# Query projections of an attention block in six groups of 8 or 12 heads instead of eight groups of 8

## The chip, the cores and the metric

The kernel runs on one core of one Trainium2 chip (trn2). The metric is the time of one execution on the device, in microseconds (us), as the median of repeated runs.

## The reference

A layer norm, sliding-window attention over a cache, and a gated FFN are combined. x has 2048 rows of 448.

```python
xn = layernorm(x)
q = (xn @ wq)                          # 448 -> 16 heads x 256
k, v = last 512 rows of the cache      # 8 key/value heads, each used by 2 query heads
s = softmax(q k^T / 16) v @ wo         # attention, 4096 -> 448
g = silu((gelu(xn @ w_gate) * (xn @ w_up)) @ w_down)
out = x + s * g
```

The rows are handled in four chunks of 512, so attention is 4 x 16 = 64 "chunk heads" (called heads below). The contraction of the projections is 448 = 3 x 128 + 64.

## The kernel before

Everything is laid out so that TensorE never waits. The gate and up matmuls of the FFN come first. Attention then alternates between *projection phases*, which make queries for a group of heads, and a *stream* in which each head's scores are followed by the P·V product of the head two places earlier.

The projections use **half-height** matmuls: two of them, on rows 0 to 63 and 64 to 127 of the array, run at the same time into two banks of PSUM, the memory that matmuls write to. This avoids padding 448 to 512. Scores, P·V, output projection and down projection use the full 128 rows.

```python
HG = 8                                   # heads of a group
# half-height pairs: u picks the rows 0-63 or 64-127, j the bank
for u, j in ((0, ph), (1, 1 - ph)):
    rows = slice(R * u, R * u + R)       # R = 64
    l = wr[rows] if k == NK else w(j, k)[rows]
    lst.append((bank[b + j][:, lo:hi], l, xnT[rows, k, cols], ...))
# ...
for c in range(NQC):                     # 4 chunks
    for g in range(NG):                  # 2 groups of 8 heads
        h0 = g * HG
        # ... (set-up at the very first group)
        for i in range(0, HG, 2):        # projection phase
            q_group(c, h0 + i, (cur, nxt)[i // 2 % 2])
        # ... (buffers released after the very first phase)
        for i in range(HG):              # stream
            s_mm(h0 + i)                 # scores, exponentials, transposes of one head
            # ... (down projections of the last two chunks at the very first heads)
            if len(late) == LAG:         # LAG = 2
                pv(late.pop(0))          # P.V of the head two back
            # ... (output projection of the last chunk after the second head of a chunk)
            late.append(h0 + i)
```

Queries lie in 8 slots (`qT`) of 2 KB per partition. The softmax of a head is 4 exponentials on ScalarE, 4 reciprocals and 4 scalings on VectorE, and 2 DMA transposes of the probabilities (`pT<-pn`).

The softmax here doesn't subtract the row's maximum and nothing guards it: scores larger than these inputs give would overflow.

## Time and profile before

| | |
|---|---|
| time, median (6 runs) | 557.23 us (556.96 to 557.56) |
| span of the profiled run | 555.1 us |
| first instruction to first query matmul | 114.035 us |
| first query matmul to start of the last output-projection matmul | 437.474 us |
| rest | 3.577 us |

The last three rows are differences of start times in the trace; "rest" runs to the end of the span. From the profile page, here are the head, the slices of TensorE and its clock, and the chain of waits:

```profile
span 555.1 us, 9781 instructions
...
PE 549.7 (99%) x3651; PEld 260.1 (47%) x3651; DVE 317.0 (57%) x817; ACT 273.9 (49%) x727; POOL 32.9 (6%) x64
...
PE   8999999999999999999999999999999999999997
...
PEclk9999999999999999999999999999999999999999
...
PE 98%; DVE 0%; DMA 0%; issue 0%
```

TensorE bounds the kernel. But "busy" cannot show how much of that time is useful: a 128x512 matmul lasts 379 ns in the trace and the next one starts well before it ends. These are three of its largest groups in attention (busy us, mean ns of one, idle before it):

```profile
L327 PE MATMUL bank<-kT,qT 128*128 128x512 bf16 x512 | 121.0, 379 | 0.0
L327 PE MATMUL bank<-pT,va 128*128 128x512 bf16 x512 | 120.8, 379 | 0.0
L327 PE MATMUL bank<-xnT,wq 64*128 64x512 bf16 x768 | 94.7, 376 | 0.0
```

All report an idle time of 0.0, also the first matmuls of a phase. The starts tell more. This is the timeline of TensorE around one projection phase (start us, length us, instruction, how many), cut in its middle:

```profile
168.13 1.89 PE L327 MATMUL bank<-kT,qT 128*128 128x512 bf16 x8
169.86 1.89 PE L327 MATMUL bank<-pT,va 128*128 128x512 bf16 x8
171.68 0.82 PE L327 MATMUL bank<-xnT,wq 64*128 64x512 bf16 x6
...
182.49 1.46 PE L327 MATMUL bank<-xnT,wq 64*128 64x512 bf16 x12
183.88 1.90 PE L327 MATMUL bank<-kT,qT 128*128 128x512 bf16 x8
185.61 1.67 PE L327 MATMUL bank<-pT,va 128*128 128x512 bf16 x7
```

Subtract the start of one line from the start of the next. Eight score matmuls take 169.86 - 168.13 = 1.73 us, 216 ns each. (The Trainium skill, "TensorE: Matmul & The Clock Gate", section "Wait — 56ns, not 53.3ns?", gives N / 2.4 GHz + about 2.5 ns for N columns, and 215.7 ns as measured at 512; this trace agrees, with 215.83 ns over 125 steps, from 184.3 to 211.3 us.) The eight P·V matmuls before the projection take 171.68 - 169.86 = 1.82 us, so 0.09 us is lost. The last 12 half-height matmuls are 6 pairs and should take 6 x 0.216 = 1.30 us; they take 183.88 - 182.49 = 1.39 us, so another 0.09 us is lost. About 10 ns more goes at the second matmul after each change. The whole is 213 or 214 ns at every phase but the first, which comes after other half-height matmuls and loses 105 ns at its exit only.

### The profile page before, as it was taken

Reading aid. Unit: us, or ns where it says so; the run is one execution under the profiler, and the core shown is the slowest. Engines: PE = TensorE matmul, PEld = TensorE weight load, DVE = VectorE, ACT = ScalarE, POOL = GpSimd, SP = SyncE. Lnnn points to the kernel's source line nnn. Section 1 sums busy time; section 2 is a strip of 40 time slices with the busy share of each in tenths; the row PEclk is TensorE's granted clock in tenths of the full one; section 3 lists DMA queues with packets and bytes.
Section 4 is the critical chain, followed back from the end, with each engine's and each line's share of the span. In section 5 each row is a group of like instructions: output and inputs, shape, how many; then the busy total and the mean of one; then the engine's idle time right before and its main releaser. Section 6 shows DMA issues by size and latency. Waiting matters only on the chain.

```text
span 555.1 us, 9781 instructions
## 1 busy us (share of the span) xinstructions
PE 549.7 (99%) x3651; PEld 260.1 (47%) x3651; DVE 317.0 (57%) x817; ACT 273.9 (49%) x727; POOL 32.9 (6%) x64
## 2 busy tenths in 40 slices
PE   8999999999999999999999999999999999999997
PEld 6444444444544444454444445544444454444455
DVE  6773534443485785525858752285785525858722
ACT  5432324353485784505758751085784504758600
POOL 1120830000000000000000000000000000000000
PEclk9999999999999999999999999999999999999999
DMA  9560799703175383313706803176364313707601
GB/s 302 104 164 9 199 277 297 108 1 39 38 134 96 76 149 81 76 35 90 153 20 152 152 21 74 34 145 100 77 151 77 77 34 90 153 20 152 153 8 34
DMA packets 163599, 57.63 MB, mean 104 GB/s; under 512 B 151456, under 2 KB 160672, under 8 KB 163552
## 3 DMA queue, kind: packets, MB, share of 16 engines
q1 hardware_dynamic: 159488, 45.16, 39.9%
q0 software_dynamic: 3296, 11.27, 6.9%
q8 instruction: 29, 0.48, 0.4%
q10 hardware_dynamic: 768, 0.57, 0.3%
q14 instruction: 18, 0.15, 0.1%
HBM read 17.92 MB, written 1.84 MB: 36 GB/s over the span
## 4 chain that ended last, share of the span: by engine, by line
PE 98%; DVE 0%; DMA 0%; issue 0%
PE bank L327 98%; DMA x<-in_A_x_dram 0%; DVE stats L375 0%; PE bank L426 0%; DVE xn L401 0%; DVE mv L378 0%; PE bank L445 0%; DVE tmp L679 0%; DVE ofin L682 0%; DVE rstd L395 0%
## 5 line engine op out<-in xcount | busy, mean ns | idle before, releaser
L640 ACT ACTIVATE p<-bank 128x512 f32<-128x512 f32 x256 | 149.5, 597 | 103.0 <-PE bank L327 99.9
L644 DVE TENSOR_SCALAR pn<-p,rden 128x512 bf16<-128x512 f32 x256 | 124.5, 486 | 16.4 <-DMA pT<-pn 7.6
L327 PE MATMUL bank<-kT,qT 128*128 128x512 bf16 x512 | 121.0, 379 | 0.0
L327 PE MATMUL bank<-pT,va 128*128 128x512 bf16 x512 | 120.8, 379 | 0.0
L327 PE MATMUL bank<-wo,oT 128*128 128x448 bf16 (+2 forms) x544 | 97.7, 341 | 0.0
L327 PE MATMUL bank<-xnT,wq 64*128 64x512 bf16 x768 | 94.7, 376 | 0.0
L327 PE MATMUL bank<-xnT,wgu 64*128 64x512 bf16 (+1 forms) x780 | 83.6, 347 | 0.4 <-issue 0.3
L327 PEld LDWEIGHTS bank<-pT,va 128*128 128x128 bf16 x512 | 50.0, 98 | 60.5 <-DMA pT<-pn 0.7
L327 PEld LDWEIGHTS bank<-kT,qT 128*128 128x128 bf16 x512 | 49.5, 98 | 61.6 <-issue 3.4
L327 PEld LDWEIGHTS bank<-wo,oT 128*128 128x128 bf16 x544 | 52.0, 98 | 45.5
L626 DVE CAST qT<-bank 128x512 bf16<-128x512 f32 x64 | 42.8, 691 | 49.4 <-PE bank L327 49.4
L321 ACT ACTIVATE qT<-bank 128x512 bf16<-128x512 f32 x64 | 38.2, 597 | 61.1 <-PE bank L327 59.5
L327 PEld LDWEIGHTS bank<-xnT,wq 64*128 64x128 bf16 x768 | 36.8, 94 | 46.8 <-ACT p L640 2.1
L321 ACT ACTIVATE gl<-bank 128x512 bf16<-128x512 f32 x56 | 33.1, 597 | 49.8 <-PE bank L327 46.6
L494 DVE TENSOR_TENSOR actT<-bank,gl 128x512 bf16<-128x512 f32 x56 | 37.8, 689 | 34.0 <-PE bank L327 25.3
L327 PEld LDWEIGHTS bank<-xnT,wgu 64*128 64x128 bf16 x780 | 35.3, 94 | 39.0 <-issue 1.3
L643 DVE RECIPROCAL rden<-rsum 128x1 f32<-128x1 f32 x256 | 40.3, 157 | 21.9 <-ACT p L640 21.8
L640 ACT ACTIVATION_READ_ACCUMULATOR p<-bank 128x1 f32 x256 | 52.8, 206 | 0.0
L679 DVE SCALAR_TENSOR_TENSOR tmp<-bank,g 128x448 f32<-128x448 f32 (+2 forms) x17 | 10.1, 596 | 72.2 <-PE bank L327 72.2
L663 DVE CAST oT<-bank 128x512 bf16<-128x512 f32 x64 | 43.7, 683 | 6.9 <-PE bank L327 6.9
L327 PE MATMUL bank<-wd,actT 128*128 128x448 bf16 x224 | 43.0, 353 | 0.0
L321 ACT ACTIVATE oT<-bank 128x512 bf16<-128x512 f32 x64 | 39.2, 612 | 7.0 <-PE bank L327 7.0
(39 smaller groups left out, 183.6 us busy)
## 6 DMA issues: line engine op xcount, KB each, us to landing
wo<-in_A_wo_dram POOLq DMA_DIRECT2D x4, 896.0 KB, 21.0
wq<-in_A_wq_dram POOLq DMA_DIRECT2D x2, 1536.0 KB, 11.4
va<-in_A_v_cache_dram POOLq DMA_DIRECT2D x8, 256.0 KB, 16.6
pT<-pn SPq DMA_TRANSPOSE x128, 2.8
xr<-in_A_x_dram POOLq DMA_DIRECT2D x16, 112.0 KB, 2.3
out_dram<-ofin SPq DMA_DIRECT2D x15, 112.0 KB, 1.7
wd<-in_B_w_down_dram SPq DMA_DIRECT2D x1, 1568.0 KB, 8.3
x<-in_A_x_dram SPq DMA_DIRECT2D x2, 448.0 KB, 5.5
```

What stands on the lines that cost most here:

```text
L321: K.op("act", lambda e, o=o, i=i: e.activation(o, i, func, scale=scale), reads, writes)
L327: ins = e.matmul(o, lhsT=l, rhs=r, start=st, stop=sp)
L494: K.op("dve", lambda e: e.tensor_tensor(actT[:, c % 2, f, :], bank[b + 1], gl[:, s, :], ALU.mult), (b_ps[b + 1], b_gl[s]), (b_actT[c % 2][ ...
L626: K.op("dve", lambda v, s=s, b=b: v.tensor_copy(qT[:, s, 1, :], bank[b + 1]), (b_ps[b + 1],), (b_qT[s][1],))
L640: K.op("act", lambda e, b=b, r=r, z=z: e.activation(p32[:, z, :], bank[b], ACT.Exp, scale=att_scale, accum_out=rsum[:, r:r + 1]), (b_ps[b] ...
L643: K.op("dve", lambda e, r=r: e.reciprocal(rden[:, r:r + 1], rsum[:, r:r + 1]), (b_rsum[r],), (b_rden[r],))
L644: K.op("dve", lambda e, r=r, z=z, y=y, t=t4 % 2: e.tensor_scalar(pn[:, y, t, :], p32[:, z, :], rden[:, r:r + 1], None, op0=ALU.mult), (b_p ...
L663: K.op("dve", lambda v, i=i, b=b: v.tensor_copy(oT[:, i, :], bank[b]), (b_ps[b],), (b_oT[i],))
L679: K.op("dve", lambda e: e.scalar_tensor_tensor(out=tmp[:, s, c0:c1], in0=bank[b][:, c0:c1], scalar=0.5, in1=g2[:, t, c0:c1], op0=ALU.mult, ...
```

## The change

The intent was one stream of 64 heads through all chunks. With 12 slots, groups may cross the border between chunks, and there are fewer of them: 8, 12, 12, 12, 12, 8. The four new slots lie on activations of the FFN that have been used by then.

```diff
+    QS = 12
 ...
-        qT, a, at = place("qT", [P, HG, 2, QC], BF16, at=b_gl[0].lo)
+        qT, a, at = place("qT", [P, QS, 2, QC], BF16, at=b_gl[0].lo - (QS - HG) * 2 * QC * 2)
 ...
-        def qs(h):
-            return HG - 1 - h % HG
+        def qs(n):
+            return QS - 1 - n % QS
 ... (q_group, s_mm and pv take the number of the head in the stream)
-        for c in range(NQC):
-            for g in range(NG):
 ...
+        NS = NQC * Hq
+        groups = [0, HG] + list(range(HG + QS, NS, QS)) + [NS]
+        K.reuse([b for y in b_qT[QS - HG:] for b in y])
 ...
+        for m in range(NS):
+            if m in groups:
+                for i in range(m, groups[groups.index(m) + 1], 2):
+                    q_group(i, (cur, nxt)[i // 2 % 2])
 ...
+            s_mm(m)
+            if m < LAG:
+                down(NQC - LAG + m, nxt)
+                if m == LAG - 1:
+                    K.reuse(b_oT + [b for y in b_qT[:QS - HG] for b in y])
+            if len(late) == LAG:
+                pv(late.pop(0))
+            if m > Hq and m % Hq == LAG - 1:
 ...             (output projection of the last chunk, as before)
+            late.append(m)
```

## The prediction

> **What bounds the kernel now.** TensorE. In the table by 10 us windows it is busy for all of every window from 20 to 550 us, at a granted clock of 1.00; the chain of waits is 98% matmuls. Since matmuls overlap, busy alone is weak evidence, so I took start-to-start distances from the timeline. In the stream of scores and P·V, eight 128x512 matmuls take 1.73 us, 216 ns each, one head 3.45 us, and nothing is lost between heads. A projection of queries for 8 heads is 112 half-height matmuls, 56 pairs of 216 ns, 12.08 us.
>
> The only regular loss in attention is at the ends of such a projection. The last P·V matmul before it is followed after 312 ns, not 216, and the step out to the scores loses about as much again. Summed from the last P·V matmul to the second score matmul, 7 of the 8 projections exceed 216 ns per matmul or pair by 215 to 216 ns in all. The first loses 105 ns only, since half-height gate and up matmuls precede it. So regular a loss is no wait for data. It fits the Trainium skill, "TensorEngine Tiling (Array Packing)", Key Properties: changing the tiling mode drains the array. The projection is 64 rows high, everything around it 128.
>
> **What the change does.** Matmuls, evictions, exponentials and transposes stay; only order and slots differ. Eight projection phases (8 heads each) become six (8, 12, 12, 12, 12, 8): two round trips of mode are removed. Nothing is added. Output projections stay after heads 17, 33 and 49. The four extra slots lie on the end of the FFN's activations and are first written for heads 8 to 11, after both last down projections, so nothing new waits.
>
> **On the critical path.** All of it: 2 x 0.216 = 0.43 us. Longer streams have no idle time to fill: TensorE has no other holes there.
>
> Could streams of 12 heads (41 us) fall behind? Per head, ScalarE does 4 exponentials of 0.60 us and a copy of 0.61, VectorE 4 x (0.16 + 0.49) + 0.68 = 3.3 us, the transposes about 2 x 1.25 us of issue, all below 3.45. From 184 to 211 us ScalarE waits about 0.54 us for TensorE at nearly every head, early and late, so no backlog grows. One late transpose (2.46 us of issue, 5.1 to land) cost TensorE 95 ns at 378 us and was soon made up.
>
> **Predicted time:** 557.23 - 0.43 = 556.8 us; 8 in 10 between 556.2 and 557.5. Faster by over 2%: 0.5%; within 2%: 98.5%; slower by over 2%: 1%.
>
> **What would show it right or wrong.**
> - The span falls by 0.3 to 0.6 us; matmul counts and means stay.
> - Six projection phases; those of 12 heads last 84 pairs x 216 ns = 18.1 us; each of five loses 216 ns at its two ends.
> - In streams of 12 heads eight matmuls still take 1.73 us at the twelfth. VectorE's waits for transposes (7.6 us before) stay of that size and do not reach TensorE.
> - Wrong, if the wait list has TensorE or its weight loads waiting for transposes, exponentials or query copies for whole microseconds, most likely late in a stream or after the second projection.
>
> **What would make it wrong.** Backlog in the softmax chain in longer streams; an order of slots that makes query copies wait; late transposes becoming commoner; or the loss at a phase's ends growing with its length. A gain above 1 us would mean a loss that start-to-start distances don't show me.

## The result and the profile after

The median is 556.86 us (556.47 to 557.55, 6 runs) against 557.23. The ratio is 0.9994, with a 95% interval of 0.9981 to 1.0007. A ratio here is the mean time of one kernel's runs over the mean of the other's in the same rounds, so it is not quite the ratio of the medians. The times by themselves do not separate the two kernels; the traces do.

| from the traces, us | before | after | difference |
|---|---|---|---|
| start to first query matmul | 114.035 | 114.105 | +0.070 |
| first query to last output-projection matmul | 437.474 | 437.008 | -0.466 |
| rest | 3.577 | 3.585 | +0.008 |
| span | 555.086 | 554.698 | -0.388 |

The same parts of the page after the change:

```profile
span 554.7 us, 9768 instructions
...
PE 547.6 (99%) x3626; PEld 260.6 (47%) x3651; DVE 317.1 (57%) x817; ACT 274.1 (49%) x727; POOL 32.9 (6%) x64
...
PE   8999999999999999999999999999999999999997
...
PEclk9999999999999999999999999999999999999999
...
PE 97%; DMA 1%; ACT 1%; issue 0%; DVE 0%; SPq 0%
```

and the three groups:

```profile
L328 PE MATMUL bank<-pT,va 128*128 128x512 bf16 x512 | 120.8, 379 | 0.0
L328 PE MATMUL bank<-kT,qT 128*128 128x512 bf16 x487 | 117.8, 379 | 2.0 <-ACT qT L322 1.0
...
L328 PE MATMUL bank<-xnT,wq 64*128 64x512 bf16 x768 | 94.4, 376 | 0.0
```

Here lies a trap. The score matmuls seem to have become 25 fewer, and TensorE seems to wait 1.0 us for query copies (`qT`). Neither is so. Weight loads (PEld) are 3651 in both kernels, and at each of the 25 places the distance of two neighbours is exactly one matmul longer (216 ns): 25 records are missing from this trace. One of them is the first score matmul after each projection phase, which shows here (timeline of TensorE):

```profile
168.20 1.89 PE L328 MATMUL bank<-kT,qT 128*128 128x512 bf16 x8
169.93 1.89 PE L328 MATMUL bank<-pT,va 128*128 128x512 bf16 x8
171.75 0.82 PE L328 MATMUL bank<-xnT,wq 64*128 64x512 bf16 x6
...
188.60 1.46 PE L328 MATMUL bank<-xnT,wq 64*128 64x512 bf16 x12
190.22 1.67 PE L328 MATMUL bank<-kT,qT 128*128 128x512 bf16 x7 [0.16 <-ACT qT L322]
191.73 1.46 PE L328 MATMUL bank<-pT,va 128*128 128x512 bf16 x6
```

and its weight load is there, at 189.99 us, one of eight (timeline of the weight loads):

```profile
189.99 1.41 PEld L328 LDWEIGHTS bank<-kT,qT 128*128 128x128 bf16 x8 [0.42 <-issue]
```

From 188.60 to 190.22 are 1.62 us: 6 pairs, one matmul without a record, and the same 0.1 us of loss. A phase of 12 heads costs the same at its ends as one of 8: 212 to 214 ns for each of five phases, once the missing record is counted. Two such phases are gone: 2 x 0.2135 = 0.427 us.

The other thing that moves TensorE in attention is a stray wait for a late transpose. The waits of VectorE and of the weight loads for transposes, before:

```profile
DVE pn L644 <- DMA pT<-pn: 7.6, 7, 1.7
PEld bank L327 <- DMA pT<-pn: 0.7, 2, 0.4
```

and after (us in total, how often, longest):

```profile
DVE pn L645 <- DMA pT<-pn: 8.1, 8, 1.3
PEld bank L328 <- DMA pT<-pn: 0.7, 3, 0.4
```

Weight loads run ahead of matmuls, so most of this never reaches TensorE. What does is a P·V matmul that starts late, as here in the kernel before (timeline of the weight loads):

```profile
378.08 0.98 PEld L327 LDWEIGHTS bank<-pT,va 128*128 128x128 bf16 x6 [0.42 <-DMA pT<-pn]
```

That is 0.105 us in all before (at 378 us) and 0.066 us after (at 437 us). The account of attention is then 0.427 + (0.105 - 0.066) = 0.466 us, and 0.466 us was measured.

### The profile page after: what moved, and what is told of

Its sections match the earlier page's. It is cut to its first block, busy times and chain, and to the rows that moved or that the text cites. A ratio compares the mean times of both kernels' runs of the same rounds, so it can differ in the third digit from the quotient of the medians.

```text
span 554.7 us, 9768 instructions
## 1 busy us (share of the span) xinstructions
PE 547.6 (99%) x3626; PEld 260.6 (47%) x3651; DVE 317.1 (57%) x817; ACT 274.1 (49%) x727; POOL 32.9 (6%) x64
## 4 chain that ended last, share of the span: by engine, by line
PE 97%; DMA 1%; ACT 1%; issue 0%; DVE 0%; SPq 0%
PE bank L328 97%; DMA x<-in_A_x_dram 1%; ACT qT L322 1%; SPq L316 0%; DVE stats L376 0%; ACT xnT L322 0%; DVE tmp L679 0%; ACT ve L392 0%; DVE ofin L682 0%; PE bank L427 0%; DVE mv L379 0%
## 5 line engine op out<-in xcount | busy, mean ns | idle before, releaser
L328 PE MATMUL bank<-kT,qT 128*128 128x512 bf16 x487 | 117.8, 379 | 2.0 <-ACT qT L322 1.0
```

The lines of the kernel that those rows point to most:

```text
L328: ins = e.matmul(o, lhsT=l, rhs=r, start=st, stop=sp)
```

## The experiments

The theory: **a change between half-height and full-height matmuls costs TensorE a fixed time of about 107 ns (half of 213 to 214; the expectations say 108), and the gain is the number of changes taken away.** Rivals: the ends of a phase lose time by waiting for banks, copies or the softmax chain; long streams are what helps; the gain is noise.

Since times spread by about 1 us in a session, each run is also read in its trace, from the first query matmul to the last output-projection matmul. The diffs are shortened: "..." marks a cut, comments after # are added, and short loops stand on one line. This table puts all runs together. "Phases" are those between full-height matmuls, without the first. "Stray" is the sum of the late starts at P·V matmuls and the step after each. "Rest" is attention minus stray, minus 0.2135 for each such phase, minus 0.105 for the first phase's exit:

| run | phases | attention us | stray us | rest us |
|---|---|---|---|---|
| before | 7 | 437.474 | 0.105 | 435.77 |
| after | 5 | 437.008 | 0.066 | 435.77 |
| after_again | 5 | 436.941 | 0 | 435.77 |
| g8 | 7 | 437.854 | 0.484 | 435.77 |
| uneven8 | 7 | 437.518 | 0.148 | 435.77 |
| g4 | 14 | 439.231 | 0.368 | 435.77 |
| g2 | 28 | 441.806 | 0 | 435.72 |
| full_q | 0 | 436.128 | 0.357 | 435.77 |
| merge_down | 5 | 437.190 | 0.245 | 435.77 |
| micro | 5 | 437.007 | 0.063 | 435.77 |
| five_phases | 4 | 436.869 | 0.140 | 435.77 |
| after_third | 5 | 438.007 | 1.061 | 435.77 |

(full_q has no change of height inside attention, so nothing is taken off for phases or exit; its trace lacks the record of the first query matmul, so 0.216 us was added to the 435.912 us that the records span.) One loss per phase explains attention to within 0.01 us in 436 in every kernel but g2. There the loss per phase is a little smaller, 211 to 213 ns, and 28 of them make the 0.05 us. In every trace the stray starts are at weight loads whose wait the timeline puts down to a transpose.

### after_again: the yardstick

No edit: the changed kernel again.

> The changed kernel once more, as the yardstick of the other runs of this call. Mode theory (each projection phase between full-height matmuls costs TensorE 0.216 us): 0.43 us below the kernel before (ratio 0.9992), with 5 rounds perhaps just clear of noise. Rival, noise or chance of that session: no difference.

Measured: 556.90 us (5 runs) against 557.30; ratio 0.9992 (0.9980 to 1.0005). The median difference of 0.40 us is as expected, but the interval still holds 1.

### full_q: the same phases without a change of height

```diff
-            group(units, 0, QC, True, True)
+            for ph in (0, 1):
+                for (b, w, wr, cols, reads, rreads, xts) in units:
+                    lst = [(bank[b + ph], w(ph, k), xnT[:, k, cols], k == 2, ph == 1 and k == 0) for k in (2, 1, 0)]
+                    if ph == 0:
+                        lst.append((bank[b], wr, xnT[:, NK, cols], False, True))
+                    mms(lst, ...)
```

> The changed kernel with the query projection in full-height 128-row matmuls: 7 per head in place of 14 half-height ones, the same 7 x 216 ns of TensorE time, the same banks, waits, evictions, phases. The result is wrong on purpose (the last 64 rows of the product are summed into one of the two halves of each head). Mode theory: 10 of the 11 single mode changes of attention vanish, so about 10 x 0.108 = 1.1 us less than the changed kernel, and the start-to-start distance at the ends of a phase is 216 ns. Rival (a phase's ends lose time by waiting for banks, copies of queries or the softmax chain): the ends still lose about 216 ns a phase, and the time is that of the changed kernel within 0.3 us.

Measured: 555.73 us against 556.90 for after_again in the same rounds, so -1.17 us; against the kernel before the ratio is 0.9973 (0.9960 to 0.9985). The comparison with the reference still passed, presumably because x outweighs s * g in the output; the mathematics is wrong all the same, and this is no version to use. Timeline of TensorE at the two ends of the second phase:

```profile
169.87 1.89 PE L328 MATMUL bank<-pT,va 128*128 128x512 bf16 x8
171.60 0.81 PE L328 MATMUL bank<-xnT,wq 128*128 128x512 bf16 x3
...
188.43 1.46 PE L328 MATMUL bank<-xnT,wq 128*128 128x512 bf16 x6
189.73 1.89 PE L328 MATMUL bank<-kT,qT 128*128 128x512 bf16 x8
```

171.60 - 169.87 = 1.73 us and 189.73 - 188.43 = 1.30 us: nothing is lost at either end. The phases, evictions and banks are as in the changed kernel; what differs is the height, and that the two banks of a head are filled one after the other. This rules out waits at the ends of a phase as the cause. Summed in the trace, the loss of 5 x 0.2135 us and the 0.105 us at the first exit are gone from attention. One change has moved: it now lies between the gate and up matmuls and the first query matmul. From the 301st gate or up matmul to the first query matmul this run takes 87.548 us (the missing record allowed for), against 87.44 us in the runs named under "merge_down", 0.11 us more.

### g4 and g2: more phases

```diff
-        groups = [0, HG] + list(range(HG + QS, NS, QS)) + [NS]
+        groups = [0] + list(range(HG, NS, 4)) + [NS]                  # g4
+            elif m % 2 == 0 and HG <= m + 2 < NS:                     # g2
+                q_group(m + 2, (cur[1], nxt[0]))
```

> The changed kernel with projection phases of 8 and then fourteen times 4 heads: 15 phases in place of 6. Mode theory: 9 x 0.216 = 1.9 us more than the changed kernel, 1.5 us more than before. Rival (long streams without a projection help by letting the softmax chain run, short ones hurt): another size than 216 ns a phase, growing where streams are 4 heads long, with waits of TensorE other than at the ends. Noise: no difference.

> The changed kernel with a first phase of 8 and then twenty-eight times 2 heads, each projected two heads ahead of its use into four banks that are free by then: 29 phases in place of 6. Mode theory: 23 x 0.216 = 5.0 us more than the changed kernel (0.9%). If evictions now hold TensorE up, more than that, and then seen as waits inside the phase or at the first scores, not as 96 ns distances.

Measured: g4 558.52 us, 1.62 us above after_again (1.9 expected); ratio to before 1.0019 (1.0006 to 1.0033). g2 561.48 us, 4.58 us above after_again (5.0 expected); ratio to before 1.0074 (1.0062 to 1.0087). Both are clear of noise. In the traces attention grew by 2.29 us and 4.87 us against after_again. Of the 2.29, 9 phases make 1.92 and a stray wait 0.37. Streams of 4 or 2 heads show no other loss, so the length of a stream does not matter. The medians of time grew by less than the traces did. In g2 the first query matmul of the profiled run happens to come 0.62 us earlier than in after_again (113.707 against 114.329 us); the rest is of the size of the spread described under "after_third".

### g8 and uneven8: the rest of the change without fewer phases

```diff
-        groups = [0, HG] + list(range(HG + QS, NS, QS)) + [NS]
+        groups = list(range(0, NS + 1, HG))                  # g8
+        groups = [0, 8, 20, 24, 36, 40, 52, 56, NS]          # uneven8
```

> The changed code and its 12 slots, but groups of 8 heads as before: 8 phases. Mode theory: the time and the spans of the kernel before, within 0.2 us. If the slots' new place or the rewritten loop matters by itself, it shows here as a difference from before.

> The changed kernel with groups of 8, 12, 4, 12, 4, 12, 4, 8 heads: 8 phases as before, but streams of 12 heads. Mode theory: only the number of phases counts, so the time of the kernel before within 0.2 us, and attention 0.43 us longer than in the changed kernel. Rival (long streams are what helps): at or below the changed kernel's time where the streams are long, or different losses at phases of 4 and of 12.

Measured: g8 556.90 us and uneven8 556.88 us against 557.25 for before in the same rounds; ratios 0.9991 (0.9978 to 1.0004) and 0.9993 (0.9979 to 1.0007). By time alone the theory would have missed here: both should have had the time of before within 0.2 us, and both medians are some 0.36 us lower, just where the changed kernel lies. The traces say otherwise. Each of the seven phases loses 212 to 214 ns in both, a phase of 4 heads like one of 12, and "rest" is that of before. The lower medians are within noise, whose interval is +-0.7 us. So the 0.37 us between the medians of before and after is not evidence for the cause either; it agreed with the prediction partly by luck.

### merge_down: one round trip less in the FFN

```diff
-        DOWN_AT = {NF + 5: 0, 2 * NF + 1: 1}
+        DOWN_AT = {2 * NF + 1: (0, 1)}
-                down(DOWN_AT[n + 1], cur)
-                cur, nxt = nxt, cur
+                for c in DOWN_AT[n + 1]:
+                    down(c, cur)
+                    cur, nxt = nxt, cur
 ... (actT as a ring of 2 * NF + 4 blocks)
```

> The changed kernel with the down projections of chunks 0 and 1 of the FFN (full-height) put together after the first blocks of chunk 2, so that the half-height gate and up matmuls are interrupted once in place of twice (activations in a ring of 32 blocks in place of 28). No other difference. Mode theory, carried to another stage: one round trip less, 0.2 us less than the changed kernel, 0.6 us less than before. Rival (the loss belongs to attention's waits): the changed kernel's time.

Measured: 556.80 us against 557.25 for before, ratio 0.9990 (0.9977 to 1.0003), unclear by time. In the trace, from the 301st recorded gate or up matmul to the first query matmul, this run takes 87.229 us; before, after and the seven other runs with two interruptions and complete records of this stretch take 87.439 to 87.442 us. That is 0.21 us less, the loss of one round trip, in a stage that has no softmax, no transposes of probabilities and no query copies. The end of one such interruption, in the changed kernel (timeline of TensorE):

```profile
73.77 1.11 PE L328 MATMUL bank<-wd,actT 128*128 128x448 bf16 x5
74.81 0.82 PE L328 MATMUL bank<-xnT,wgu 64*128 64x512 bf16 x6
```

Five down matmuls of 448 columns, 189 ns each elsewhere, should take 0.95 us and take 1.04: the same 0.09 us.

### micro: the change of height by itself

```diff
+        for n in (QC, P):                       # 512, then 128 columns
+            for i in range(32): full(n)         # independent matmuls, results unread
+            for i in range(32): half(n)         # pairs
+            for i in range(32):
+                full(n); half(n)
```

> The changed kernel with independent matmuls appended after TensorE's last one, results unread: 32 full-height, then 32 half-height pairs, then 32 times one full-height and one pair in turn, first with 512 columns, then with 128. No waits are possible in them. Mode theory: with 512 columns the grouped 64 take 13.8 us and the 64 in turn 13.8 + 64 x 0.108 = 20.7 us; with 128 columns 3.6 us and, if the loss is a fixed time whatever the columns, 3.6 + 6.9 = 10.5 us; if it scales with the columns, 5.3 us. Rival (no cost of a mode change by itself): in turn takes as long as grouped.

Measured: 603.87 us in all (2 runs). The table by windows has one row for each block, in the order of the program: 32 full, 32 pairs, 64 in turn, with 512 columns; then the same with 128 columns, of which the last is given in two parts, without the 0.4 us between them (us; busy time and count, which includes a few matmuls that overlap the borders; clock; DMA share; GB/s):

```profile
core 0: us, PE busy (x), PEclk, DMA share, GB/s
551.05:558.05 7.00, 7.00 (x35) 1.00 0.06 18
558.05:565.06 7.01, 7.01 (x65) 1.00 0.01 2
565.06:585.68 20.62, 20.62 (x98) 1.00 0.00 0
585.68:587.58 1.90, 1.90 (x35) 1.00 0.05 9
587.58:589.47 1.89, 1.89 (x66) 1.00 0.00 0
589.47:595.80 6.33, 6.33 (x63) 1.00 0.01 3
596.20:601.10 4.90, 4.90 (x36) 0.50 0.00 0
```

Grouped, 64 steps of 512 columns take 7.00 + 7.01 = 14.0 us, with two changes in them. In turn they take 20.62 us, 322 ns a step in place of 216: **106 ns a change**. With 128 columns a step in turn takes 162 ns (39 steps from 589.47 to 595.80 us), against 56 ns grouped: again 106 ns a change. The cost is a fixed time at both widths, and no wait is involved: the list of TensorE's waits is empty over this stretch. TensorE is "busy" all the while, which is why no idle time ever showed this loss. The 128-column block in turn then met a clock of 0.50, so the 10.5 us predicted for the whole block holds for its rate only until 596 us.

### five_phases: the theory used for a version

```diff
+        groups = [0, 8, 20, 32, 48, NS]
 ... (from head 32 on, four more slots in the transposed inputs of chunks 0 and 1)
 ... (on top of merge_down)
```

> The kernel with merged down projections, and four more query slots from head 32 on (in the columns of the transposed inputs of chunks 0 and 1, whose last projection is then done), so groups of 8, 12, 12, 16, 16 heads: 5 phases. Mode theory, by the trace: attention 0.216 us less than the changed kernel apart from stray waits for late transposes (0 to 0.5 us in a run so far), the stage of gate, up and down 0.210 us less as in the merged run. By time, 0.4 us below the changed kernel and 0.85 us below before (ratio 0.9985), which five rounds should hold just clear of 1. Rival (only long streams matter, or the gain is noise): no step of 216 ns for the phase taken away.

Measured: 555.98 us (5 runs) against 556.98 for before, ratio 0.9983 (0.9970 to 0.9996), and against 556.93 for the changed kernel in the same rounds. The result is right (same operations, other slots). It is the only correct version here whose interval against before lies wholly below 1, at -0.2%. In the trace, attention has one phase less ("rest" is unchanged), and gate, up and down take 87.227 us in place of 87.44. The 0.95 us between the medians is more than the 0.43 us that theory gives; the surplus is noise as far as the traces tell.

### after_third, and where the spread of times comes from

> The changed kernel once more, beside the run above: 0.43 us below before by theory; its earlier medians lay 0.37 and 0.4 us below.

Measured: 556.93 us (6 runs) against 556.98; ratio 1.0005 (0.9988 to 1.0022). The expected 0.43 us does not show in these times. One of the six runs took 559.55 us, and it happens to be the profiled one. Its timeline early in the FFN:

```profile
12.87 0.29 PE L328 MATMUL bank<-xnT,wgu 64*128 64x128 bf16 x4
15.07 0.23 PE L328 MATMUL bank<-xnT,wgu 64*128 64x128 bf16 x2 [1.91 <-issue]
```

The same place in uneven8:

```profile
12.48 0.42 PE L328 MATMUL bank<-xnT,wgu 64*128 64x128 bf16 x6
12.74 0.22 PE L328 MATMUL bank<-xnT,wgur 64*128 64x128 bf16 x2
```

The same six matmuls come in one piece here and in two pieces, 2.2 us apart, in after_third.

At one point near 12.5 us TensorE stops for 0.06 us (uneven8), 0.40 (after), 0.50 (before), 0.84 (g4) or 2.07 us (after_third), inside one chain of matmuls with no semaphore in it. The first query matmul starts between 113.69 and 116.18 us, the latest in the run with the longest stop; the stop is only part of that (after_again has none, and starts at 114.33 us). This and the stray waits for transposes (0 to 1.06 us a run) can be larger than the effect under study, and they came with both kinds of kernel. Why it stops there is not settled: the profile names no wait. The 12 traces point one way, though. In 11 the stop comes after the same matmul, and the next one starts 2.3 to 2.7 us after a 16 KB packet begins on the instruction queue, whether that packet comes at 9.99 us (g8, a stop of 0.15 us) or at 12.34 us (after_third). In after_again it came 3.2 us before, and there is no stop. So TensorE probably waits there for its own instructions; no run tested it.

## Why the prediction was right

- **The bound and the place of the loss** were right. TensorE takes all of attention, and the only regular loss is at the ends of a projection phase. full_q removes it without touching phases or waits; micro produces it without phases or waits.
- **The mechanism**: the Trainium skill, "TensorEngine Tiling (Array Packing)", Key Properties, says that changing the tiling mode drains the array. The runs agree that a change has a fixed cost. They do not show that it is a drain rather than, for instance, weight loads that cannot run ahead across the change. In the kernel before, a weight load normally starts one matmul ahead of its use; at a change it starts only with its own matmul, 304 to 308 ns after the previous matmul's start. That part stays open, and the saving does not depend on it.
- **The size**: 2 x 0.216 us. The traces show 0.427 us, and 0.466 us for attention with the stray waits. The predicted 556.8 us met 556.86 us, but the spread of runs means that this agreement of medians proves little; g8 met the same median without the saving.
- **No backlog in streams of 12**: right. Eight matmuls still take 1.73 us, and VectorE's waits for transposes went from 7.6 to 8.1 us.
- **A point that was off**: the prediction said that such waits do not reach TensorE. They do, a little, before and after the change, when a transpose is late: between 0 and 1.06 us in a run. It knew one such case, of 95 ns, and called it "soon made up". TensorE does not make it up: it takes all of attention, and "rest" comes out alike only with these waits taken off in full. Also "matmul counts stay" holds for the weight loads; the matmul records themselves were 25 short.
- **"The loss growing with the phase's length"**, named as a danger, is excluded: phases of 2, 4, 8, 12 and 16 heads all lose 211 to 214 ns.

## What to carry to other kernels

When TensorE is "busy" all the time, measure start-to-start distances, and look at the seams where the shape of matmuls changes; a loss there shows as no idle time and no wait. Each change between half-height and full-height matmuls cost about 106 to 107 ns here, so it pays to batch work of one height, up to what the buffers hold; count the changes before you write the code, since a few of them are worth only tenths of a microsecond. When an effect is smaller than the spread of runs, add up the trace by stage against a count, and test the cause with a kernel in which it is multiplied.

## What the Trainium skill lacked or had wrong

- "TensorEngine Tiling (Array Packing)", Key Properties, says that a change of mode drains, but gives no size. Here a change between 64-row and 128-row matmuls cost 106 ns with 512 columns and with 128 (micro), and 211 to 214 ns for a round trip in the kernel.
- "TensorE: Matmul & The Clock Gate", Back-to-back issue gap, says that in a real kernel matmuls of 512 columns come every 131 ns or so and that 216 ns over-counts. In this real kernel full-height ones come every 215.83 ns, with a weight load each, for over a hundred in a row. Only half-height pairs come at 108 ns per matmul.
- The same page, Part 3, The mechanism, says in its list that weight loads overlap matmuls in flight only when the row group differs, though the paragraph above the list also allows it for loads to the background weight buffer. The "only" does not hold here: full-height loads overlap full-height matmuls throughout: a load from 171.157 to 171.255 us lies inside the matmul from 171.156 to 171.535 us (before). Across a change of height they do not run ahead: 304 to 308 ns after the last start.
- No page that I found says that a profile can lack single matmul records whose weight loads are there, or how to notice it: 25 of 512 score matmuls in after, none in before, with a false wait of 1.0 us for query copies as the result.
